# A long convolution in four FFT stages ahead of a wide MLP: an intermediate re-laid in blocks of four columns, the third stage one chunk later, deeper product buffers, one store for each tile of y

## The chip, the core and the metric

The kernel runs on one core of a Trainium2 chip. The metric is device microseconds of one execution; the median of three runs is compared. Engines: PE does matrix products (PEld is its weight load, which can run beside a product), DVE, ACT and POOL do elementwise work, SP issues all DMAs of this kernel in one queue. [...]

## The reference

```python
def _attn_ref(x, v, pos_emb, w1, w2):          # x, v: 4 x 12480 x 128
    h_mlp = np.maximum(pos_emb @ w1, 0.0) @ w2
    h_filt = h_mlp * np.exp(-0.01 * pos)[:, None]
    u = x * v
    Uf = np.fft.rfft(u, n=2 * S, axis=1)
    Hf = np.fft.rfft(h_filt, n=2 * S, axis=0)
    y = np.fft.irfft(Uf * Hf[None], n=2 * S, axis=1)[:, :S]
    return x * y

def _moe_ref(x, w_in, w_out):                  # w_in: 128 x 2048, w_out: 2048 x 128
    h = x @ w_in
    g = h * np.clip(h + 3.0, 0.0, 6.0) / 6.0
    return g @ w_out
```

The second function gets the output of the first. All of it is float32.

## The kernel before

The FFT of 12544 = 64 x 196 points is done as matrix products. The work falls into a filter part (the spectrum of h, kept in DRAM as `hd`), eight **periods** (one for each group g of 2 batches x 32 channels), a **last turn**, and the MLP ("MoE" in the code) over 98 tiles of 512 positions.

Each period works on a tensor `z` of 128 partitions x 99 frequencies (K2) x 128 columns; there are two, `z[0]` and `z[1]`, used by even and odd groups. The stages:

- **First stage** (L282, copied out by ACT at L294): 16 products for four columns, written to `z[:, :, col:col+4]`. A **visit** does four of these, 16 columns, for the group after the present one.
- **Second stage** (L301): 4 frequencies are one **chunk** (25 in a period, c = 0 to 24); the table `tab` is the stationary operand, `z[:, k, :]` the moving one.
- **Products**: ACT copies a swapped half (L499, L500), DVE multiplies by the filter spectrum `h` (L520 to L523) and POOL adds (L527) into the tile `pa`. POOL also multiplies x and v (L453).
- **Third stage** (L542, copied out by ACT at L550): the products of a chunk with the same `tab`, written back into `z[:, k, :]`. It follows the products by `LAG` chunks.
- **Back** (L557): four columns of `z` are transposed on PE; here `z[:, :, col]` is the stationary operand and the identity the moving one. ACT copies the result to `w` (L560). 32 backs of group g-1 lie in period g.
- **Fourth stage** (L574): for 16 columns, from `w`; ACT copies one half (L584), DVE makes `y` from both (L586), SP stores `y` to `yd` and two single rows to `ye` (L592, L595).

Every engine works in the order in which the program is written (`manual_schedule`). In a period, `chunk` issues products of c, third stage of c-LAG+1, the load of a later `tab` into the buffer that the third stage freed, and the second stage of c+1; then follow one or two backs, in most periods with steps of a decode of the MLP's weights on DVE (`weight`), and after each fourth back a fourth stage and a visit. The fourth stage pops the oldest entry of `pend`, so it is one group of 16 columns behind the backs; the one left over runs in chunk 0 of the next period. The tables have `NT` buffers, the spectra `h` four. `z` is copied out of the single PSUM bank `s3`; backs, first and fourth stages share four banks `ts`.

The MLP loads its tiles with two DMAs, `xt` and `yt` (L713, L728), multiplies them (L741), transposes on DVE, and runs six products for each of 16 blocks; L768 to L770 are the first layer, L803 to L807 the second.

Of the kernel before, what the change touches and what calls it, by code (L numbers as in the profile page):

```python
# [9 lines left out]
F32 = mybir.dt.float32  # L10
# [27 lines left out]
G = 32  # L38
# [22 lines left out]
LAG = 3  # L61
# [5 lines left out]
NT = 7  # L67
# [91 lines left out]
@with_exitstack  # L159
def hyena_moe(ctx, tc, x, v, xt, pos_emb, w1, w2, w_in, w_out, c_tab, d_tab, f_tab, g_tab, win_d, ident_d, out):  # L160
    nc = tc.nc
    P = 128

    dram = ctx.enter_context(tc.tile_pool(name="dram", bufs=1, space=DRAM))
    hd = [dram.tile([D // G // 2, P, K2, 2, G], F32, name=f"hd{h}") for h in range(2)]
    yd = [[dram.tile([NR, 4, 32, G // GH, N1, GH], F32, name=f"yd{b}_{k}") for k in range(2)] for b in range(B)]
    ye = dram.tile([len(REST), D // GH, N1, GH], F32, name="ye")
    wd = [dram.tile([2, P, DFF], F32, name=f"wd{i}") for i in range(2)]
    w_in = w_in.bitcast(I32).rearrange("p (q k c) -> q p k c", k=NW, c=2)
    w_out = w_out.bitcast(I32).rearrange("(q f p) (k c) -> q p f k c", f=NW // D, p=P, c=2)  # L170
    weights = [(w[q], wd[i][:, :, q * NW : (q + 1) * NW]) for i, w in enumerate((w_in, w_out)) for q in range(DFF // NW)]

    const = ctx.enter_context(tc.tile_pool(name="const", bufs=1))
    ident = const.tile([P, P], F32, name="ident")

    left, right = ExitStack(), ExitStack()
    with tc.manual_schedule():
        conv = Conv(tc, nc, left, right, x, v, c_tab, d_tab, g_tab, ident, hd, yd, ye, weights)
# [5 lines left out]
        moe = Moe(ctx, tc, nc, xt, wd, yd, ye, out)  # L184
        conv.last_turn(moe)
        right.close()
        moe.run()
# [64 lines left out]
class Conv:  # L252
    def __init__(self, tc, nc, left, right, x, v, c_tab, d_tab, g_tab, ident, hd, yd, ye, weights):
        self.tc, self.nc, self.left, self.right = tc, nc, left, right
        self.x, self.v, self.g_tab, self.ident, self.hd, self.yd = x, v, g_tab, ident, hd, yd
        self.c_tab, self.d_tab, self.weights, self.ye = c_tab, d_tab, weights, ye
# [4 lines left out]
        self.z = [self.keep.tile([128, K2, COLS], F32, name=f"z{i}") for i in range(2)]  # L261
# [12 lines left out]
    def first_stage(self, z, u, k, piece, j):  # L274
# [15 lines left out]
        dst, src = z[:, :K2, col : col + 4], tv[:, :, :K2].rearrange("p j k -> p k j")  # L290
# [5 lines left out]
    def second_stage(self, tab, z, c):  # L296
# [3 lines left out]
        for i in range(kw):  # L300
            self.nc.tensor.matmul(  # L301
                t[:, i * 128 : (i + 1) * 128], tab[:, i, :], z[:, c * CH + i, :], start=True, stop=True
            )
        return t, kw

    def filter(self, pos_emb, w1, w2, f_tab, win_d, ident_d):
        tc, nc = self.tc, self.nc
        z, ftab = self.z
# [15 lines left out]
        flat = z.rearrange("p k c -> p (k c)")  # L324
# [178 lines left out]
    def products(self, item):  # L503
# [5 lines left out]
        a = self.pr.tile([P, CH, 2 * GB, G], F32, tag="a", name="pa")  # L509
        a2 = self.pr.tile([P, CH, 2 * GB, G], F32, tag="a2", name="pa2", bufs=2)  # L510
        q = self.pr.tile([P, CH, GB, G], F32, tag="q", name="pq", bufs=2)
        q2 = self.pr.tile([P, CH, GB, G], F32, tag="q2", name="pq2", bufs=2)
# [23 lines left out]
    def third_stage(self, item):  # L536
# [13 lines left out]
        nc.scalar.copy(z[:, c * CH : c * CH + kw, :].rearrange("p k c -> p (k c)"), t[:, : kw * 128])  # L550

    def back(self, g, col):
# [11 lines left out]
    def fourth_stage(self):  # L564
# [24 lines left out]
        for h in range(2):  # L589
            e = ch // GH + h  # L590
            for i, p, q, r, n in PARTS:
                nc.sync.dma_start(self.yd[b][k][q, d // G, r : r + n, e], y[64 * h + p : 64 * h + p + n, i])  # L592
            for i, p, r in ((0, 49, 49), (1, 1, 97)):
                if r < R[k]:
                    nc.sync.dma_start(  # L595
                        self.ye[REST.index((b, k, r)), d // GH + e].unsqueeze(0), y[64 * h + p : 64 * h + p + 1, i]
                    )

    def period(self, g):
# [7 lines left out]
        for c in range(NCHUNK):  # L607
# [4 lines left out]
            while n < end:  # L612
# [4 lines left out]
                if n % VISIT == 0:  # L617
                    if n > VISIT:
                        self.fourth_stage()
                    if g + 1 < NG:  # L620
                        self.visit(g + 1, n // VISIT - 1)

    def chunk(self, g, c):
# [7 lines left out]
        if g > 1 and c == 0:  # L631
            self.fourth_stage()
# [39 lines left out]
class Moe:  # L672
# [7 lines left out]
    def __init__(self, ctx, tc, nc, x, wd, yd, ye, out):  # L680
        self.ctx, self.tc, self.nc = ctx, tc, nc
        self.x, self.yd, self.ye, self.out = x, yd, ye, out
# [26 lines left out]
    def load(self, t):  # L709
# [4 lines left out]
        if self.is_rest(t):  # L714
            i = self.tiles[t]
            s = REST.index(i[0])
            for j in range(4):
                for m in range(len(i)):
                    a = self.ye[s + m, 4 * j : 4 * j + 4].rearrange("e (h r) c -> r h e c", r=32)
# [5 lines left out]
        else:  # L725
            b, k, q, n = self.tiles[t]
            a = self.yd[b][k][q].rearrange("q r e n c -> (q r) e n c")[:, :, n : n + self.NB, :]
            nc.sync.dma_start(  # L728
                y.rearrange("p (e m) -> p e m", e=4), a.rearrange("p e n c -> p e (n c)")
            )  # L730
        self.loaded[t] = xt, y

# [142 lines left out]
```

## Time and profile before

| what | us |
|---|---|
| median of three runs (3252.92, 3256.47, 3272.07) | 3256.47 |
| the profiled execution | 3259.06 |
| its span | 3257.3 |
| PE busy in it | 3156.4 |
| DVE, ACT, POOL busy in it | 2315.7, 2356.5, 2079.7 |
| granted PE clock, mean | 0.992 |

The execution is the span and some 1.8 us around it. The filter part ends at 160.3 us, where the first period begins; the last turn ends at 1120.9, where the first product of the MLP starts. PE's share of 97% is a mean over these parts, which have different limits.

### The profile page before, as it was taken

To read this page: it belongs to the slowest core of one execution; us is meant where nothing else is said; L and a number is where in the kernel's file an instruction comes from. 1 tells how busy PE (TensorE), PEld (TensorE's weight loads), DVE (VectorE), ACT (ScalarE), POOL (GpSimd) and SP (SyncE) were. 2 spreads that over 40 slices of the span, in tenths; PEclk is the share of its full clock that TensorE was granted. 3 is DMA by queue.
4 is the path that set the end of the run, shared out by engine and by line. 5 is a ranking of instruction groups with operands and counts; after the bars stand their busy time and mean duration, and the time that the engine had idled before them with its cause. 6 is when DMAs were issued, how large, how long until landed. Compare 5 with 4: busy or idle time off the path is not lost.

```text
span 3257.3 us, 53858 instructions
## 1 busy us (share of the span) xinstructions
PE 3156.4 (97%) x20026; PEld 2667.5 (82%) x20026; DVE 2315.7 (71%) x2691; ACT 2356.5 (72%) x3039; POOL 2079.7 (64%) x1242
## 2 busy tenths in 40 slices
PE   9989899899899899999999999999999999999999
PEld 8988787787787588888888888888888888888887
DVE  4456676676656377777777777777777777777776
ACT  2356666666676577778877787778777877787777
POOL 1177767767767166666666666666666666666666
PEclk9999999999999999999999999999999999999999
DMA  6677777777765401011111111111111110111010
GB/s 232 198 202 193 206 194 196 206 200 193 203 173 168 141 30 39 30 36 39 39 39 34 36 39 39 33 36 40 39 30 39 39 39 30 39 39 39 30 39 23
DMA packets 236980, 296.70 MB, mean 91 GB/s; under 512 B 38727, under 2 KB 159854, under 8 KB 235694
## 3 DMA queue, kind: packets, MB, share of 16 engines
q1 hardware_dynamic: 236718, 293.26, 31.7%
q8 instruction: 158, 2.59, 0.3%
q14 instruction: 104, 0.85, 0.1%
HBM read 224.87 MB, written 68.29 MB: 90 GB/s over the span
## 4 chain that ended last, share of the span: by engine, by line
PE 66%; DMA 1%; SPq 0%; POOL 0%; ACT 0%; issue 0%; DVE 0%; DVEq 0%; ACTq 0%
PE acc L807 11%; PE acc L803 11%; PE acc L804 11%; PE ph L769 11%; PE ph L770 11%; PE ph L768 11%; DMA yd<-y 1%; PE ts L574 0%; PE ts L557 0%; SPq L592 0%; PE s L557 0%; DMA yt<-yd 0%; PE s L542 0%; PE s L301 0%; DMA ye<-y 0%; DMA tab<-in_g_tab 0%
## 5 line engine op out<-in xcount | busy, mean ns | idle before, releaser
L792 POOL TENSOR_TENSOR glo<-g,ghi 128x1024 fp32r<-128x1024 f32 x588 | 1404.3, 2396 | 775.4 <-ACT ghi L790 775.2
L780 DVE SCALAR_TENSOR_TENSOR g<-r,ph 128x1024 f32<-128x1024 f32 (+1 forms) x784 | 949.3, 1211 | 413.8 <-ACT r L778 413.6
L778 ACT ACTIVATE r<-ph,three 128x1024 f32<-128x1024 f32 (+1 forms) x784 | 871.4, 1112 | 277.6 <-PE ph L770 277.5
L790 ACT CAST ghi<-g 128x1024 fp32r<-128x1024 f32 (+1 forms) x784 | 811.1, 1035 | 5.4 <-DMA ye<-y 4.2
L768 PE MATMUL ph<-xhi,win_hi 128*128 128x512 f32 (+1 forms) x1568 | 609.1, 388 | 2.3 <-DVE y L586 2.3
L803 PE MATMUL acc<-ghi,wout_hi 128*128 128x512 f32 (+1 forms) x1568 | 608.6, 388 | 2.3 <-ACT ghi L790 2.3
L769 PE MATMUL ph<-xlo,win_hi 128*128 128x512 f32 (+1 forms) x1568 | 608.8, 388 | 0.0
L770 PE MATMUL ph<-xhi,win_lo 128*128 128x512 f32 (+1 forms) x1568 | 608.8, 388 | 0.0
L804 PE MATMUL acc<-ghi,wout_lo 128*128 128x512 f32 (+1 forms) x1568 | 608.6, 388 | 0.0
L807 PE MATMUL acc<-glo,wout_hi 128*128 128x512 f32 (+1 forms) x1568 | 481.8, 388 | 1.0 <-POOL glo L792 1.0
L527 POOL TENSOR_TENSOR pa<-pa,pq 128x256 f32<-128x256 f32 (+1 forms) x400 | 290.3, 732 | 247.4 <-DVE pa L521 220.8
L768 PEld LDWEIGHTS ph<-xhi,win_hi 128*128 128x128 f32 x1568 | 294.7, 188 | 64.2 <-issue 2.7
L803 PEld LDWEIGHTS acc<-ghi,wout_hi 128*128 128x128 f32 x1568 | 294.7, 188 | 63.4 <-ACT ghi L790 2.8
L807 PEld LDWEIGHTS acc<-glo,wout_hi 128*128 128x128 f32 x1568 | 294.0, 188 | 62.4 <-POOL glo L792 2.0
L770 PEld LDWEIGHTS ph<-xhi,win_lo 128*128 128x128 f32 x1568 | 294.6, 188 | 60.7
L804 PEld LDWEIGHTS acc<-ghi,wout_lo 128*128 128x128 f32 x1568 | 294.6, 188 | 60.6
L769 PEld LDWEIGHTS ph<-xlo,win_hi 128*128 128x128 f32 x1568 | 294.6, 188 | 60.5
L792 DVE TENSOR_TENSOR glo<-g,ghi 128x1024 fp32r<-128x1024 f32 x196 | 283.3, 1446 | 0.0
L520 DVE TENSOR_TENSOR pq<-s,h 128x256 f32<-128x256 f32 (+1 forms) x200 | 84.1, 420 | 280.0 <-POOL pa L527 124.3
L542 PE MATMUL s<-pa,tab 128*128 128x128 f32 x1694 | 242.3, 289 | 40.5 <-POOL pa L527 30.3
L542 PEld LDWEIGHTS s<-pa,tab 128*128 128x128 f32 x1694 | 212.4, 197 | 64.4 <-POOL pa L527 50.0
L741 DVE TENSOR_TENSOR xy<-xt,yt 128x512 f32<-128x512 f32 x96 | 260.3, 2711 | 0.0
(60 smaller groups left out, 3675.4 us busy)
## 6 DMA issues: line engine op xcount, KB each, us to landing
tab<-in_g_tab SPq DMA_DIRECT2D x192, 256.0 KB
h<-hd SPq DMA_DIRECT2D x384, 128.0 KB
xt<-in_xt SPq DMA_DIRECT2D x98, 256.0 KB
out<-o SPq DMA_DIRECT2D x97, 256.0 KB
xt<-in_x SPq DMA_DIRECT2D x64, 384.0 KB
vt<-in_v SPq DMA_DIRECT2D x64, 384.0 KB
yt<-yd SPq DMA_DIRECT2D x96, 256.0 KB
yd<-y SPq DMA_DIRECT2D x256, 64.0 KB
```

What stands on the lines that cost most here:

```text
L527: nc.gpsimd.tensor_tensor(out=x, in0=x, in1=y, op=add)
L542: nc.tensor.matmul(t[:, i * 128 : (i + 1) * 128], tab[:, i, :], a[:, i].rearrange("p s g -> p (s g)"), start=(n == 0), stop=(n == len(term ...
L768: nc.tensor.matmul(ph[:, i, :ne], self.win_hi[:, sl], hi[:, :ne], start=True, stop=False)
L769: nc.tensor.matmul(ph[:, i, :ne], self.win_hi[:, sl], lo[:, :ne], start=False, stop=False)
L770: nc.tensor.matmul(ph[:, i, :ne], self.win_lo[:, sl], hi[:, :ne], start=False, stop=True)
L778: nc.scalar.activation(r[:, :, :ne], ph[:, :, :ne], AF.Relu, bias=self.three)
L780: nc.vector.scalar_tensor_tensor(out=g[:, :, :ne], in0=r[:, :, :ne], scalar=6.0, in1=ph[:, :, :ne], op0=ALU.min, op1=ALU.mult)
L790: nc.scalar.copy(ghi[:, :, :ne], g[:, :, :ne])
L792: e.tensor_tensor(out=glo[:, :, :ne], in0=g[:, :, :ne], in1=ghi[:, :, :ne].bitcast(F32), op=ALU.subtract)
L803: nc.tensor.matmul(a, self.wout_hi[:, f, :], ghi[:, i, :ne], start=(f == 0), stop=False)
L804: nc.tensor.matmul(a, self.wout_lo[:, f, :], ghi[:, i, :ne], start=False, stop=False)
L807: nc.tensor.matmul(a, self.wout_hi[:, f, :], glo[:, i, :ne], start=False, stop=(f == NFC - 1))
```

## The change

- `z` has the shape 128 x 32 blocks x 99 frequencies x 4 columns. A column's 99 values, which the back loads as weights, lie 16 bytes apart and not 512; a frequency's 128 values, which the second stage reads and the third stage's copy writes, lie in 32 runs of four floats (16 for the copy of four frequencies) and not in one row. The first stage's copy writes one run of 396 floats.
- `LAG` is 4, not 3, and there are 8 tables, not 7. The product buffers `a2`, `q`, `q2` have three copies and not two, `a` four and not three; `w` has two and not three.
- The visit comes ahead of the fourth stage, the fourth stage runs from the first 16 columns on, and none is left for chunk 0 of the next period. In period 7, which has no visit, the fourth stage follows its last back directly.
- `y` is stored whole by one DMA, in the order in which it lies; `ye` is gone. The MLP gathers a tile of `yd` with four or eight DMAs of 32, 17 or 15 rows and not one of 128.

```diff
-LAG = 3
+LAG = 4
...
-NT = 7
+NT = 8
...
-    yd = [[dram.tile([NR, 4, 32, G // GH, N1, GH], F32, name=f"yd{b}_{k}") for k in range(2)] for b in range(B)]
-    ye = dram.tile([len(REST), D // GH, N1, GH], F32, name="ye")
+    yd = [[dram.tile([D // G, G // GY, 2 * 64, 2, N1, GH], F32, name=f"yd{b}_{k}") for k in range(2)] for b in range(B)]
...
-        self.z = [self.keep.tile([128, K2, COLS], F32, name=f"z{i}") for i in range(2)]
+        self.z = [self.keep.tile([128, COLS // 4, K2, 4], F32, name=f"z{i}") for i in range(2)]
...
-        dst, src = z[:, :K2, col : col + 4], tv[:, :, :K2].rearrange("p j k -> p k j")
+        dst, src = z[:, col // 4], tv[:, :, :K2].rearrange("p j k -> p k j")
...
-                t[:, i * 128 : (i + 1) * 128], tab[:, i, :], z[:, c * CH + i, :], start=True, stop=True
+                t[:, i * 128 : (i + 1) * 128], tab[:, i, :], z[:, :, c * CH + i, :], start=True, stop=True
...
-        a = self.pr.tile([P, CH, 2 * GB, G], F32, tag="a", name="pa")
-        a2 = self.pr.tile([P, CH, 2 * GB, G], F32, tag="a2", name="pa2", bufs=2)
-        q = self.pr.tile([P, CH, GB, G], F32, tag="q", name="pq", bufs=2)
-        q2 = self.pr.tile([P, CH, GB, G], F32, tag="q2", name="pq2", bufs=2)
+        a = self.pr.tile([P, CH, 2 * GB, G], F32, tag="a", name="pa", bufs=4)
+        a2 = self.pr.tile([P, CH, 2 * GB, G], F32, tag="a2", name="pa2")
+        q = self.pr.tile([P, CH, GB, G], F32, tag="q", name="pq")
+        q2 = self.pr.tile([P, CH, GB, G], F32, tag="q2", name="pq2")
...
-        nc.scalar.copy(z[:, c * CH : c * CH + kw, :].rearrange("p k c -> p (k c)"), t[:, : kw * 128])
+        nc.scalar.copy(z[:, :, c * CH : c * CH + kw, :], t[:, : kw * 128].rearrange("p (k q c) -> p q k c", k=kw, c=4))
...
-            nc.tensor.transpose(t[:K2, i * 128 : (i + 1) * 128], self.z[g % 2][:, :, col + i], self.ident)
+            nc.tensor.transpose(t[:K2, i * 128 : (i + 1) * 128], self.z[g % 2][:, col // 4, :, i], self.ident)
...
-            self.w = self.wp.tile([K2, GY, 128], F32, tag="w", name="w", bufs=3)
+            self.w = self.wp.tile([K2, GY, 128], F32, tag="w", name="w")
...
-        for h in range(2):
-            e = ch // GH + h
-            for i, p, q, r, n in PARTS:
-                nc.sync.dma_start(self.yd[b][k][q, d // G, r : r + n, e], y[64 * h + p : 64 * h + p + n, i])
-            for i, p, r in ((0, 49, 49), (1, 1, 97)):
...
+        nc.sync.dma_start(self.yd[b][k][d // G, ch // GY], y)
...
                 if n % VISIT == 0:
-                    if n > VISIT:
-                        self.fourth_stage()
                     if g + 1 < NG:
                         self.visit(g + 1, n // VISIT - 1)
+                    self.fourth_stage()
...
-        if g > 1 and c == 0:
-            self.fourth_stage()
...
             b, k, q, n = self.tiles[t]
-            a = self.yd[b][k][q].rearrange("q r e n c -> (q r) e n c")[:, :, n : n + self.NB, :]
-            nc.sync.dma_start(
-                y.rearrange("p (e m) -> p e m", e=4), a.rearrange("p e n c -> p e (n c)")
-            )
+            for i, p, block, r, m in PARTS:
+                for j in range(4 if block == q else 0):
+                    a = self.parts(b, k, j, i, p, p + m)[:, :, n : n + self.NB, :]
+                    nc.sync.dma_start(
+                        y[32 * j + r : 32 * j + r + m, :].rearrange("r (e m) -> r e m", e=4),
+                        a.rearrange("r e n c -> r e (n c)"),
+                    )
...
+    def parts(self, b, k, j, i, p0, p1):
+
+        return self.yd[b][k][j].rearrange("f (e p) i n c -> i p (f e) n c", p=64)[i, p0:p1]
```

Three places in the engines' order. First PE around one fourth stage in period 3: `s_...` is the result of a second or third stage, `pa` the products, `ts` the shared bank. Before:

```order
L557 MATMUL ts<-ident,z_79 99x128 x4
L574 MATMUL ts<-w,dtab 64x512 x4
L282 MATMUL ts<-ctab,u 64x99 x32
L557 MATMUL ts<-ident,z_79 99x128 x4
L542 MATMUL s_6905<-pa,tab 128x128 x4
```

After (the first stage is L281 there, the second L300):

```order
L557 MATMUL ts<-ident,z_78 99x128 x4
L281 MATMUL ts<-ctab,u 64x99 x32
L574 MATMUL ts<-w,dtab 64x512 x4
L542 MATMUL s_6538<-pa,tab 128x128 x4
L300 MATMUL s_6546<-z_79,tab 128x128 x4
```

The visit's products now stand between the last transposes and the fourth stage that takes their copy.

The second place is PE in period 7, the last one, around a fourth stage. Before:

```order
L301 MATMUL s_12705<-z_80,tab 128x128 x4
L557 MATMUL ts<-ident,z_79 99x128 x4
L574 MATMUL ts<-w,dtab 64x512 x4
L542 MATMUL s_12756<-pa,tab 128x128 x4
L301 MATMUL s_12764<-z_80,tab 128x128 x4
```

After:

```order
L300 MATMUL s_12230<-z_79,tab 128x128 x4
L557 MATMUL ts<-ident,z_78 99x128 x4
L574 MATMUL ts<-w,dtab 64x512 x4
L542 MATMUL s_12270<-pa,tab 128x128 x4
L300 MATMUL s_12278<-z_79,tab 128x128 x4
```

The rows look alike, but the `w` that L574 reads was filled 16 columns earlier before, and is filled by the copy of the transposes right ahead of it after; nothing else stands between.

The third place is SP around the stores of one fourth stage in a later period. Before:

```order
L471 DMA tab<-in_g_tab 128x512
L592 DMA yd_1_62<-y 32x512 x2
L592 DMA yd_1_62<-y 17x512
L592 DMA yd_1_62<-y 15x512
L595 DMA ye<-y 1x512
L592 DMA yd_1_62<-y 32x512 x2
L592 DMA yd_1_62<-y 17x512
L592 DMA yd_1_62<-y 15x512
L595 DMA ye<-y 1x512
L484 DMA h<-hd_57 64x2x256 x2
```

After:

```order
L484 DMA h<-hd_57 64x2x256 x2
L471 DMA tab<-in_g_tab 128x512
L589 DMA yd_1_62<-y 128x1024
L484 DMA h<-hd_57 64x2x256 x2
L471 DMA tab<-in_g_tab 128x512
```

Ten or twelve issues have become one.

## Rows read from the trace of the kernel before

**Rows 1.** Windows, stages: stretch, length, busy time by engine, clock, DMA share, GB/s

```profile
160.30:1120.90 960.60, 877.23 (x8398) 761.66 (x8398) 597.66 (x1106) 617.87 (x1160) 653.81 (x641) 0.98 0.71 191
1120.90:3257.30 2136.40, 2126.49 (x9409) 1760.61 (x9408) 1642.55 (x1371) 1687.37 (x1764) 1404.32 (x588) 1.00 0.12 37
```

**Rows 2.** Waits of PE from 160.3 to 1120.9: total us, times, longest

```profile
PE s L542 <- POOL pa L527: 30.3, 50, 1.8
PE s L301 <- DMA tab<-in_g_tab: 19.3, 12, 3.1
PE ts L557 <- DVE y L586: 16.0, 6, 3.5
PE s L542 <- ACT z L550: 7.6, 16, 1.5
PE s L301 <- DVE pa L521: 4.2, 2, 2.6
```

**Rows 3.** Windows: one whole period, and one stretch of lower clock

```profile
493.60:616.50 122.90, 110.79 (x1103) 97.04 (x1102) 83.53 (x149) 79.38 (x151) 86.89 (x83) 0.97 0.76 204
...
399.85:403.26 3.41, 3.37 (x16) 3.40 (x17) 3.34 (x7) 0.43 (x1) 2.80 (x3) 0.50 1.12 272
```

**Rows 4.** Timeline of PE around that stretch: start, length, idle before and its releaser

```profile
399.89 2.05 PE L301 MATMUL s<-z,tab 128*128 128x128 f32 x8 [3.10 <-DMA tab<-in_g_tab]
401.73 1.79 PE L557 MATMUL ts<-ident,z 128*99 128x128 f32 x8
...
404.25 1.06 PE L301 MATMUL s<-z,tab 128*128 128x128 f32 x8
405.14 0.84 PE L557 MATMUL ts<-ident,z 128*99 128x128 f32 x4
```

**Rows 5.** Lines by form, weight loads: busy us, mean ns, idle before

```profile
L557 PEld LDWEIGHTS ts<-ident,z 128*99 128x99 f32 x960 | 179.9, 262 | 20.7 <-DVE y L586 17.3 <-issue 1.6 <-ACT z L550 0.9
...
L357 PEld LDWEIGHTS h<-w2bd,ht 128*98 128x98 f32 x256 | 29.0, 165 | 0.4 <-issue 0.2
```

**Rows 6.** Timeline of PE in the last turn; the clock rises at 1079.1

```profile
1075.67 1.06 PE L557 MATMUL s<-ident,z 128*99 128x128 f32 x4
1076.52 1.06 PE L557 MATMUL ts<-ident,z 128*99 128x128 f32 x4
...
1081.61 0.84 PE L557 MATMUL s<-ident,z 128*99 128x128 f32 x4
1082.29 0.84 PE L557 MATMUL ts<-ident,z 128*99 128x128 f32 x4
```

**Rows 7.** Timeline of SP, stores of one fourth stage: first and last

```profile
429.05 1.58 SPq L592 DMA_DIRECT2D yd<-y  x4
...
433.66 0.51 SPq L595 DMA_DIRECT2D ye<-y  x2
```

**Rows 8.** Timeline near the end of period 3: a visit, then a wait

```profile
596.79 2.90 PE L282 MATMUL ts<-ctab,u 97*64 97x99 f32 x64
...
601.89 1.27 DVE L586 TENSOR_TENSOR y<-ts,o 128x512 f32<-128x512 f32 x2
...
603.22 0.95 PE L557 MATMUL ts<-ident,z 128*99 128x128 f32 x4 [3.53 <-DVE y L586]
```

**Rows 9.** Lines by form, copies by ACT: busy us, mean ns

```profile
L294 ACT COPY z<-ts 128x396 f32<-128x396 f32 x272 | 133.1, 489 | 96.3 <-PE ts L282 77.3 <-DMA xt<-in_x 14.9
...
L550 ACT COPY z<-s 128x512 f32<-128x512 f32 x192 | 111.9, 583 | 5.5 <-PE s L542 5.5
...
L378 ACT COPY st<-s 128x256 f32<-128x256 f32 x48 | 17.9, 372 | 41.4 <-PE s L301 30.8 <-DVE st L380 10.0 <-DMA tab<-in_g_tab 0.6
```

**Rows 10.** Timeline of PE where the MLP begins

```profile
1117.61 1.07 PE L574 MATMUL ts<-w,dtab 99*64 99x512 f32 x2 [1.82 <-ACT w L560]
...
1124.88 0.47 PE L768 MATMUL ph<-xhi,win_hi 128*128 128x512 f32 x1 [2.29 <-DVE y L586]
...
1133.00 0.50 PE L803 MATMUL acc<-ghi,wout_hi 128*128 128x512 f32 x1 [2.33 <-ACT ghi L790]
```

More of the change, by code (lines that the diff above doesn't have):

```diff
@@ L177, in hyena_moe @@
     with tc.manual_schedule():
-        conv = Conv(tc, nc, left, right, x, v, c_tab, d_tab, g_tab, ident, hd, yd, ye, weights)
+        conv = Conv(tc, nc, left, right, x, v, c_tab, d_tab, g_tab, ident, hd, yd, weights)
         conv.filter(pos_emb, w1, w2, f_tab, win_d, ident_d)
@@ L183, in hyena_moe @@
         left.close()
-        moe = Moe(ctx, tc, nc, xt, wd, yd, ye, out)
+        moe = Moe(ctx, tc, nc, xt, wd, yd, out)
         conv.last_turn(moe)
@@ L252, with __init__ @@
 class Conv:
-    def __init__(self, tc, nc, left, right, x, v, c_tab, d_tab, g_tab, ident, hd, yd, ye, weights):
+    def __init__(self, tc, nc, left, right, x, v, c_tab, d_tab, g_tab, ident, hd, yd, weights):
         self.tc, self.nc, self.left, self.right = tc, nc, left, right
         self.x, self.v, self.g_tab, self.ident, self.hd, self.yd = x, v, g_tab, ident, hd, yd
-        self.c_tab, self.d_tab, self.weights, self.ye = c_tab, d_tab, weights, ye
+        self.c_tab, self.d_tab, self.weights = c_tab, d_tab, weights
         self.loaded, self.gated, self.n_loaded = [], [], 0
@@ L307, in filter @@
         tc, nc = self.tc, self.nc
-        z, ftab = self.z
+        z = self.z[0]
+        ftab = self.z[1].rearrange("p q k c -> p (q k c)").rearrange("p (k c) -> p k c", k=K2)
         P = 128
@@ L322, in filter @@
         NB = 4
-        flat = z.rearrange("p k c -> p (k c)")
+        flat = z.rearrange("p q k c -> p (q k c)")
         pT = flat[:, : N1 * R[0]].rearrange("p (n r) -> p n r", r=R[0])
@@ L588, in fourth_stage @@
         k, b, d = self.place(g, piece)
-        for h in range(2):
-            e = ch // GH + h
-            for i, p, q, r, n in PARTS:
-                nc.sync.dma_start(self.yd[b][k][q, d // G, r : r + n, e], y[64 * h + p : 64 * h + p + n, i])
-            for i, p, r in ((0, 49, 49), (1, 1, 97)):
-                if r < R[k]:
-                    nc.sync.dma_start(
-                        self.ye[REST.index((b, k, r)), d // GH + e].unsqueeze(0), y[64 * h + p : 64 * h + p + 1, i]
-                    )
+        nc.sync.dma_start(self.yd[b][k][d // G, ch // GY], y)
     def period(self, g):
@@ L678, with __init__ @@
     NB = 16
-    def __init__(self, ctx, tc, nc, x, wd, yd, ye, out):
+    def __init__(self, ctx, tc, nc, x, wd, yd, out):
         self.ctx, self.tc, self.nc = ctx, tc, nc
-        self.x, self.yd, self.ye, self.out = x, yd, ye, out
+        self.x, self.yd, self.out = x, yd, out
         P = 128
@@ L714, in load @@
         if self.is_rest(t):
[L715 to L719, printed above, removed]
+            for m, (b, k, r) in enumerate(self.tiles[t]):
+                i, p = (0, r) if r < RH else (1, R[0] - r)
+                for j in range(4):
+                    a = self.parts(b, k, j, i, p, p + 1)[0].rearrange("e (h r) c -> r h e c", r=32)
                     for h in range(2):
@@ L726, in load @@
             b, k, q, n = self.tiles[t]
-            a = self.yd[b][k][q].rearrange("q r e n c -> (q r) e n c")[:, :, n : n + self.NB, :]
-            nc.sync.dma_start(
-                y.rearrange("p (e m) -> p e m", e=4), a.rearrange("p e n c -> p e (n c)")
-            )
+            for i, p, block, r, m in PARTS:
[5 more added lines that the diff above has]
+                    )
         self.loaded[t] = xt, y
+    def parts(self, b, k, j, i, p0, p1):
+        return self.yd[b][k][j].rearrange("f (e p) i n c -> i p (f e) n c", p=64)[i, p0:p1]
     def gate(self, t):
```

## The prediction, made before the changed kernel ran

> **What bounds the kernel now.** I read the windows by stage first. The MLP keeps PE busy 2126.5 of 2136.4 us, and none of its arithmetic is touched, so nearly all that can move lies in the 960.6 us of the periods and the last turn, where PE is busy 877.2 and idle 83.4 [rows 1]. Within a period of 122.9 us PE works 110.8, POOL 86.9, DVE 83.5, ACT 79.4, and the DMA engines are 0.76 busy, some 93 us [rows 3]. PE is the bound, with a second row of limits at 70 to 76% behind it. So a microsecond off PE's own work or off its waits shortens the run until the period comes near 93.
>
> The list of PE's waits then says what the 83.4 us are: 30.3 for the last POOL addition of a product, 19.3 for a table, 16.0 for DVE's y, 7.6 for the copy out of the single bank `s3`, 4.2 for a DVE product that still reads a second-stage bank [rows 2]. These five are 77.4 of the 83.4.
>
> The waits cost more than their length. After the 3.10 us wait for a table the granted clock is 0.50, the 1.2 GHz level, for 3.41 us [rows 3, 4]. Eight second-stage instructions take 1.84 us there (399.89 to 401.73) and 0.89 at the higher level (404.25 to 405.14) [rows 4]; four transposes take 0.85 and 0.68 [rows 6]. That stretch, eight of the one and eight of the other, cost 0.95 + 0.34 = 1.3 us. A period at a mean of 0.97 loses 3% of 122.9 us of full clock, so it has 7.4 us at the lower level, two such stretches [rows 3]. Six periods (1 to 6) read 0.97, so there are about twelve, some 16 us in all.
>
> **The third stage one chunk later, with the product buffers.** Products of c are issued ahead of third stage c-2 before, c-3 after, so POOL has one more chunk of PE time (period / 25, 4.9 us on average) to finish. The longest of its 50 waits is 1.8 us [rows 2], well under that. The added buffers are what lets DVE and POOL use the slack. I take 25 of 30.3 (15 to 30: POOL's work is not shortened, and where chunks carry no backs it can still be last). The 7.6 for `s3` stay, since that bank stays single; so do the 4.2.
>
> The moved third stage brings its copy with it. The third stage of a period's last chunk now runs in chunk 2 of the next, right ahead of the first back, which reads the copied column. Between them lies only a second stage of 0.89 us [rows 4] against a copy of up to 0.58 [rows 9] and its queue on ACT: +0.3 us in seven periods, +2 (0 to 5).
>
> **The visit ahead of the fourth stage, and no fourth stage in chunk 0.** The typical wait for y: the visit starts at 596.79 and is over at 599.7, DVE ends y at 603.16 and the next transposes, whose bank y still holds, start at 603.22 after 3.53 us idle [rows 8]. After the change the visit's 2.9 us lie ahead of the fourth stage, and two backs with a chunk behind it before such a bank comes round. DVE still has the same work there, so some of the wait can come back as one for its product: 13 of 16.0 saved (6 to 16).
>
> In periods 1 to 6 the visit covers the copy of `w` (0.59 us). In period 7 there is no visit, and eight fourth stages wait for the copy just issued. Here the last fourth stage of the last turn shows the price: 1.82 us, of which the copy is only a third, the rest ACT's queue [rows 10]. The floor is the copy, 0.6, and its signals. Queued behind the wait on PE are a third and a second stage, and POOL and DVE behind those. 1.25 us each, +10 (6 to 18).
>
> **Whole-tile stores.** The issues of one fourth stage hold SP from 429.05 to 434.17 [rows 7], and every load of `h` and `tab` behind them waits, eight times a period: 8 x 5.1 = 41 us of a period's 122.9. One issue there is 0.26 to 0.40 us (0.51 / 2, 1.58 / 4), so some 38 us of SP's time come free. The bytes stay the same, and the DMA engines at 0.76 are not relieved of them, so I take 11 of the 19.3 us for tables (4 to 19). The depth of prefetch does not change: one more table, held one chunk longer.
>
> At the MLP's start the second layer's first product waits 2.33 us for a copy by ACT [rows 10], which lies in memory that the last `y` gives up when its stores have landed, and these stores stand in SP's late queue. I take 3 us there (0 to 5); the wait of 2.29 for a PSUM bank stays. The MLP's gathers are three to seven issues more for each tile of 21.8 us (2136.4 / 98), with two tiles loaded ahead; PE's 99.5% leaves them no share: 0.
>
> **Fewer stretches at the lower clock.** With most of the waits of over 2 us gone, I take 9 of the 16 us (3 to 15).
>
> **z in blocks of four.** On the copies I put 0: 256, 396 and 512 elements take 0.372, 0.489 and 0.583 us, that is 0.82 ns for each added element [rows 9], though the middle one reads PSUM 512 bytes apart and writes in runs of four, and the other two do not. What the layout can change is the transposes. Their weight load is 99 columns that lie 512 bytes apart and takes 262 ns; 98 columns that lie in a row take 165 [rows 5]. And the transposes are held by that load: at the lower clock one takes 0.85/4 = 0.213 us, not far from a second-stage instruction (0.230), at the higher one 0.170 where that takes 0.111 [rows 4, 6]. An array at double clock would go twice as fast; something that does not follow the clock holds it at 0.170. If the load ran at the pace of one in a row, a transpose would take 0.111 and the 1024 of them would give 60 us.
>
> Does a step of 16 bytes read like one of 512, or like a row? No row shows it; both ends are 0 and 60 us. In both layouts no two of the wanted values are adjacent; adjacency is what the 165 ns load has and the 262 ns load lacks. I take the nearest row, the strided load: 0.
>
> [...]
>
> **The sum.** -25 + 2 - 13 + 10 - 11 - 3 - 9 + 0 = -49 us. The profiled execution is 3259.06, so it would be 3210; it lies 2.6 us over the median of three, so the median comes to 3256.5 - 49 = **3207 us** (-1.5%). With every term at its good end the sum is -85 + 6 = -79 (3177), at its bad end -28 + 23 = -5 (3251).
>
> **Rivals.** *The load at full pace.* The 16-byte step reads like a row. For it: it is the one thing that the new order of z changes for an operation held by its operand. Against it: above. Of the 60 us I count 50, since a period then comes to about 109 us with some 93 of DMA in it, which leaves less room for late tables: 3207 - 50 = 3157 (3147 to 3171). [...]
>
> *The waits only move.* DVE decodes weights in bursts, POOL and DMA stay as loaded as they are, and each wait that goes is replaced by the next in line. For it: five different releasers, and none of the engines does less. Against: none is over 76% in a period. Near the bad end of the sum: -5 to -25, 3240.
>
> *The second stage pays for the runs.* Its moving operand is now 32 runs of four values with jumps of 1584 bytes between them. If each run cost what a far step costs the weight load, (262 - 165) / 99 = 1 ns, an instruction would take 32 ns more; there are 1980 of them (198 in each of eight periods, 396 in the filter part), +63 us, and the time would be 3207 + 63 = 3270, slower than before. If every value paid, it would be four times that. It decides from 25 ns an instruction on (49 / 1980). Against it: nothing in the trace speaks for a price at the fourth value, and the copy by ACT in runs of four has none [rows 9].
>
> **How the numbers follow.** Chances: forecast 0.56, the load at full pace 0.29, waits only move 0.09, runs pay 0.06. A measurement of this kernel tells about 1% from no change, 33 us. Of the forecast about four fifths lie beyond that: faster 0.45 + 0.29 + 0.02 = 0.76; slower by over 1% 0.04, the dear half of the runs; within 1% 0.20. The range leaves out the lower edge of the second case and the upper tail of the others: 3147 to 3238. The forecast's own range is 3180 to 3235.
>
> **What would show it.** The weight load of L557 at 262 ns and four transposes in 0.68 us confirm the term of 0; 165 ns and 0.45 mean the first rival. The wait for POOL should be under 8 us, for y under 4, for tables under 13; new ones should stand in period 7 (L574 for ACT's copy, eight of 0.8 to 1.8 us). Period 3 should come to 115 to 117 us at a clock of 0.98 to 0.99, and the MLP begin near 1075. The second stage should keep 0.89 us for eight. The forecast is wrong if L557's load changes, if tables still wait after SP is free (then DMA bandwidth, not the queue, made them late), or if PE's wait for y comes back under DVE's products.

## The result, and the profile after

The changed kernel takes 3212.86 us (median of four runs, 3211.72 to 3214.58), the kernel before 3256.64 beside it (3252.92 to 3272.07): a ratio of **0.9857**, 95% interval [0.9825, 0.9889]. The profiled execution takes 3211.72 us, 47.3 less than the one before; the forecast of that step was 49.

The windows of the changed kernel by stage, then period 3 (columns as in [rows 1]):

```profile
159.17:1081.25 922.08, 872.49 (x8399) 754.79 (x8399) 592.69 (x1106) 610.40 (x1160) 652.96 (x641) 1.00 0.71 207
1081.25:3209.60 2128.35, 2123.59 (x9409) 1758.93 (x9408) 1640.62 (x1371) 1686.40 (x1764) 1404.15 (x588) 1.00 0.12 37
478.65:593.40 114.75, 108.81 (x1104) 95.13 (x1103) 82.13 (x150) 78.20 (x151) 86.93 (x84) 1.00 0.76 221
```

Against [rows 1] the periods and the last turn give 38.5 us and the MLP 8.1. PE's idle time there falls from 83.4 to 49.6 us (922.08 - 872.49). A period takes 114.75 for 122.9, and its clock reads 1.00 for 0.97 [rows 3]. This clock is the granted share: the traces of both kernels have two levels of it, 1.00 and 0.50. The stretches that the prediction and the expectations place at 1.2 GHz are those at 0.50; no trace shows a frequency. The DMA engines move more bytes in less time, 207 for 191 GB/s at the same share of 0.71: by the page the whole kernel moves 304.7 MB for 296.7, since a whole tile of `y` (512 KB) holds rows that the pieces left out (some 390 KB).

The waits of PE in that stretch (as in [rows 2]):

```profile
PE s L542 <- ACT z L550: 33.4, 50, 1.3
PE ts L557 <- ACT z L550: 9.0, 8, 1.3
PE s L300 <- DVE pa L521: 6.3, 7, 2.1
PE s L542 <- POOL pa L527: 0.8, 1, 0.8
```

The waits for POOL, for a table and for y are gone: 65.6 us of them but for 0.8, where the forecast had left 16.6. But the copy out of `s3`, 8.2 us before (7.6 in [rows 2] and 0.6 under L557), now holds PE for 42.4. The list of waits shows half of the waits replaced, not removed.

Where that wait sits is plain in the timeline of PE of the changed kernel, at the start of period 3:

```profile
481.00 1.06 PE L300 MATMUL s<-z,tab 128*128 128x128 f32 x8
483.11 1.13 PE L542 MATMUL s<-pa,tab 128*128 128x128 f32 x8 [1.05 <-ACT z L550]
...
486.42 0.91 PE L542 MATMUL s<-pa,tab 128*128 128x128 f32 x6 [1.28 <-ACT z L550]
...
489.53 0.99 PE L557 MATMUL ts<-ident,z 128*99 128x128 f32 x4 [1.31 <-ACT z L550]
```

ACT in the same stretch:

```profile
481.30 0.56 ACT L499 COPY sw<-s 64x512 f32<-64x512 f32 x1 [1.41 <-DVE pa L523]
481.89 0.57 ACT L500 ACTIVATE sw<-s 64x512 f32<-64x512 f32 x1
482.38 0.58 ACT L550 COPY z<-s 128x512 f32<-128x512 f32 x1
484.61 0.56 ACT L499 COPY sw<-s 64x512 f32<-64x512 f32 x1 [1.64 <-DVE pa L523]
...
487.92 0.56 ACT L499 COPY sw<-s 64x512 f32<-64x512 f32 x1 [1.64 <-DVE pa L523]
```

Read across the two. ACT's L499 starts every 3.31 us (481.30, 484.61, 487.92), each time after DVE's last product of the chunk before (L523, which reads the one `sw` bank that L499 overwrites). The copy L550 stands behind L499 and L500 in ACT's order. The next third stage needs the bank that L550 empties, so PE, which has some 2 us of work a chunk here (a third and a second stage), takes 3.3 us for it, too. These chunks have no backs or visits to fill the gap.

The new layout, lines by form (as in [rows 5, 9]):

```profile
L557 PEld LDWEIGHTS ts<-ident,z 128*99 128x99 f32 x960 | 188.9, 275 | 21.9 <-issue 11.4 <-ACT z L550 10.5
L293 ACT COPY z<-ts 128x396 f32<-128x396 f32 x272 | 132.3, 489 | 92.5 <-PE ts L281 77.2 <-DMA xt<-in_x 14.9
L550 ACT COPY z<-s 128x512 f32<-128x512 f32 x192 | 111.9, 583 | 3.9 <-PE s L542 3.9
```

PE in the last turn and at the MLP's start (as in [rows 6, 10]):

```profile
1073.57 0.89 PE L557 MATMUL ts<-ident,z 128*99 128x128 f32 x4
1074.30 0.89 PE L557 MATMUL s<-ident,z 128*99 128x128 f32 x4
...
1090.05 0.73 PE L802 MATMUL acc<-glo,wout_hi 128*128 128x512 f32 x2 [0.39 <-POOL glo L787]
```

The copies cost what they cost, to the nanosecond (489 and 583 ns in both kernels). The weight load became a little slower, 275 ns for 262, and four transposes take 0.73 us for 0.68. Where the MLP begins, the waits of 2.29 and 2.33 us [rows 10] are gone; in the kernel before, a stretch of 6.8 us at a granted clock of 0.50 (1133.7 to 1140.5) followed them, which is gone too.

Period 7, PE again, one of eight fourth stages:

```profile
965.16 2.93 PE L574 MATMUL ts<-w,dtab 99*64 99x512 f32 x8
```

SP, one store (as in [rows 7]):

```profile
365.99 0.38 SPq L589 DMA_DIRECT2D yd<-y  x1
```

The fourth stage there takes 2.93 us; with its visit ahead it takes 1.91. The one store holds SP for 0.38 us, where the twelve of [rows 7] held it for 5.1, the waits between them included.

### The profile page after: what moved, and what is told of

It reads as the page before. It is cut to its first block, busy times and chain, and to the rows that moved or that the text cites. A ratio compares the mean times of both kernels' runs of the same rounds, so it can differ in the third digit from the quotient of the medians.

```text
span 3209.6 us, 53638 instructions
## 1 busy us (share of the span) xinstructions
PE 3147.8 (98%) x20026; PEld 2658.5 (83%) x20026; DVE 2308.7 (72%) x2691; ACT 2348.0 (73%) x3039; POOL 2078.7 (65%) x1242
## 4 chain that ended last, share of the span: by engine, by line
PE 68%; ACT 0%; DVE 0%; POOL 0%; DMA 0%; issue 0%; ACTq 0%; DVEq 0%
PE acc L802 11%; PE acc L798 11%; PE acc L799 11%; PE ph L763 11%; PE ph L765 11%; PE ph L764 11%; PE ts L574 1%; PE ts L557 1%; PE s L557 0%; PE s L542 0%; PE s L300 0%; DMA yd<-y 0%; POOL glo L787 0%; ACT z L550 0%; DVE y L586 0%
## 5 line engine op out<-in xcount | busy, mean ns | idle before, releaser
L542 PEld LDWEIGHTS s<-pa,tab 128*128 128x128 f32 x1694 | 205.9, 192 | 80.7 <-POOL pa L527 42.4
L542 PE MATMUL s<-pa,tab 128*128 128x128 f32 x1694 | 233.9, 282 | 34.2 <-ACT z L550 33.4
L527 POOL TENSOR_TENSOR pa<-pa,pa 128x512 f32<-128x512 f32 (+1 forms) x186 | 236.7, 1273 | 14.6
```

Source lines behind the costliest of these rows:

```text
L527: nc.gpsimd.tensor_tensor(out=x, in0=x, in1=y, op=add)
L542: nc.tensor.matmul(t[:, i * 128 : (i + 1) * 128], tab[:, i, :], a[:, i].rearrange("p s g -> p (s g)"), start=(n == 0), stop=(n == len(term ...
```

## The experiments

Four parts were changed: layout, third stage (with buffers), order, stores. The first question is which of them carries the 47 us. Times are medians, each with its ratio to the kernel before on the same chip. The diffs are cut to the lines that name the edit; the lines that follow from it are left out.

**One part alone, on the kernel before.** The layout:

```diff
-        self.z = [self.keep.tile([128, K2, COLS], F32, name=f"z{i}") for i in range(2)]
+        self.z = [self.keep.tile([128, COLS // 4, K2, 4], F32, name=f"z{i}") for i in range(2)]
```

> The kernel before with the new layout of z alone. Theory (the near step costs 12 ns a transpose): 3257 + 12 = 3269 us (3262 to 3274), load of L557 275 ns. Rival (the step is not the cause): 3257 (3253 to 3261), load 262. Whichever holds, the 33 us and more that the change gave don't come from the layout: if they did, this run would be at 3215.

3261.46 us, 1.0002 [0.9992, 1.0011]. The load is 275 ns here too, and the transposes work some 10 us longer, but PE idles 4.5 us less; the time does not move. So the load is the theory's and the time, within its interval, the rival's.

The stores:

```diff
-                nc.sync.dma_start(self.yd[b][k][q, d // G, r : r + n, e], y[64 * h + p : 64 * h + p + n, i])
...
+        nc.sync.dma_start(self.yd[b][k][d // G, ch // GY], y)
```

> The kernel before with nothing but the whole-tile stores of y, without the tensor of single rows, and the MLP gathers that go with them. The changed kernel with the old stores stood at 1.0006, so the other three parts together gave nothing there. Theory: these parts shift the bound to the tables, which come late only under the old stores, so the stores alone remove what is late for that reason and leave the waits of the rest: table waits 19.3 to under 3 us, ghi at the MLP's start 2.3 to about 1, POOL's 30 and y's 16 stay, about half of the 48 us at 1.2 GHz goes: ratio 0.989 to 0.993. Rival: the stores are the whole change, and worth the same 48 us here: ratio 0.984 to 0.987.

3214.72 us, **0.9857** [0.9842, 0.9872]: the number of the rival, and the whole gain of the change. Windows by stage:

```profile
160.36:1084.78 924.42, 869.80 (x8399) 753.58 (x8399) 599.02 (x1106) 615.34 (x1160) 654.62 (x641) 0.99 0.72 207
1084.78:3213.13 2128.35, 2123.37 (x9409) 1759.26 (x9408) 1640.79 (x1371) 1687.36 (x1764) 1405.05 (x588) 1.00 0.12 37
```

PE's waits in the first of them (lines are one lower here):

```profile
PE s L541 <- POOL pa L526: 26.4, 46, 1.8
PE s L541 <- ACT sw L498: 13.8, 6, 2.3
...
PE ts L556 <- DVE y L585: 4.5, 10, 0.9
```

The table waits are gone (19.3 before), POOL's stay as the theory had it, and the MLP part is as short as in the changed kernel. What the theory had wrong is y: 16.0 fell to 4.5 with PE's order untouched. In the kernel before, DVE's own waits in these parts show y held back 19.8 us in five places by earlier stores that still held its tile; here it has none:

```profile
DVE y L586 <- DMA yd<-y: 16.3, 4, 6.7
DVE y L586 <- DMA ye<-y: 3.5, 1, 3.5
```

The third stage:

```diff
-LAG = 3
+LAG = 4
...
-NT = 7
+NT = 8
```

> The kernel before with nothing but the third stage three chunks behind the products, eight tables, and the new numbers of product buffers and of w. Taking this part out of the changed kernel cost 0.9939 against 0.9857, 27 us. Theory: under the old stores PE that no longer waits for POOL runs into late tables: POOL's waits fall from 30 to under 4 us, those for a table rise from 19 to over 28, ratio 0.997 to 1.003. Rival: the part is worth its 27 us by itself: ratio 0.990 to 0.993, waits for a table at 19 or less.

3254.65 us, 0.9985 [0.9974, 0.9996], as the theory said. The three main waits of PE:

```profile
PE s L301 <- DMA tab<-in_g_tab: 30.8, 19, 3.1
PE s L542 <- ACT z L550: 16.4, 35, 1.3
PE ts L557 <- DVE y L586: 12.3, 6, 3.2
```

POOL's 30.3 us are down to 0.8, and 11.5 of them came back as later tables, 15.3 as waits for the s3 copy (23.5 with the 7.1 that stand under L557, for 8.2).

**One part taken out of the changed kernel.** The stores:

```diff
-        nc.sync.dma_start(self.yd[b][k][d // G, ch // GY], y)
+                nc.sync.dma_start(self.yd[b][k][q, d // G, r : r + n, e], y[64 * h + p : 64 * h + p + n, i])
```

> The changed kernel with the old stores of y in pieces, the single rows in a tensor of their own, and the old gathers of the MLP; everything else stays changed. Theory: the ten issues of each fourth stage made the tables late, and the long waits for tables are what lowered the granted clock. Then waits for a table come back to 12 to 25 us, several stretches at 1.2 GHz with them (20 us or more in all), and the MLP's start gets its 2 us wait for ghi back: ratio 0.991 to 0.997 (changed kernel 0.9857). Rival: DMA bandwidth and the depth of prefetch made them late, so that the eighth table is what removed the waits: ratio 0.985 to 0.988, waits for tables under 5 us.

3263.58 us, **1.0006** [0.9996, 1.0016], beyond what the theory allowed: without the stores the other three parts together give nothing. No wait for y is left here, under the old stores. The longest row of PE's waits (lines are one higher here):

```profile
PE s L301 <- DMA tab<-in_g_tab: 34.8, 19, 3.7
```

SP ahead of two late tables:

```profile
366.69 1.47 SPq L593 DMA_DIRECT2D yd<-y  x4
...
369.88 0.54 SPq L472 DMA_DIRECT2D tab<-in_g_tab  x1
...
375.60 0.34 SPq L472 DMA_DIRECT2D tab<-in_g_tab  x1
```

PE where it uses them:

```profile
372.97 1.13 PE L301 MATMUL s<-z,tab 128*128 128x128 f32 x8 [0.91 <-DMA tab<-in_g_tab]
...
378.77 2.05 PE L301 MATMUL s<-z,tab 128*128 128x128 f32 x8 [3.60 <-DMA tab<-in_g_tab]
```

There are 200 issues of a table and 200 second stages, in the same order. By that count the table used at 378.77 was issued at 375.60, and the one at 372.97 at 369.88: PE takes a table as soon as it lands, about 3 us after its issue. From the end of the issue to the use it is never under 6.6 us in the changed kernel and as short as 2.5 here (periods 1 to 7), though there are eight tables in both; with the stores alone, and seven tables, it is never under 6.4. So the late tables come from the place in SP's queue, not from the depth of prefetch or from bandwidth.

The queue lost more than the time of the issues. From the first period to the MLP the stores of `y` hold SP for 223 us in the kernel before and for 23 in the changed one. Besides, the list of SP's waits before has 132 us (194 waits) in which SP stands until an earlier transfer has landed, often one that the store behind it does not need; with the changed kernel it is 20 us (31 waits), with the stores alone 25. In the run here one of 1.4 us, for an `xt`, stands right ahead of the issue at 375.60. The longest row of the kernel before:

```profile
SPq L592 <- DMA vt<-in_v: 24.5, 25, 1.8
```

Why a store waits for the landing of `vt` is not shown. Nor does a run keep the many issues but store the tile in its new place, so that the number of issues and the new form of the stores are not told apart.

The third stage:

```diff
-LAG = 4
+LAG = 3
...
-NT = 8
+NT = 7
```

> The changed kernel with the third stage two chunks behind the products again, seven tables and the old numbers of product buffers; layout, order of visit and fourth stage, and stores stay changed. Theory: the later third stage only exchanged one wait for another (POOL 30.3 to 0.8 us, copy out of s3 8.2 to 42.4), because ACT's copies of the swapped half and DVE's products form a loop of 3.3 us a chunk that bounds PE there whatever stands behind. Then POOL's waits come back to 20 to 30 us, the waits for the s3 copy fall under 15, and the time stays within 0.3% of the changed kernel: ratio to before 0.983 to 0.989 (changed kernel 0.9857). Rival, the prediction's own term: it is worth 23 us, ratio 0.992 to 0.994, with the waits for the s3 copy still near 40.

3240.02 us, 0.9939 [0.9924, 0.9954]. The time is the rival's, the prediction's own term; the waits for POOL and for the s3 copy are much as the theory had them, not near 40 for the copy as the rival had. PE's waits:

```profile
PE s L542 <- POOL pa L527: 32.6, 37, 1.8
PE s L542 <- ACT z L550: 15.0, 27, 1.2
PE s L542 <- ACT sw L499: 13.5, 6, 2.3
```

The theory fails as a mere exchange because a wait for `sw` stands here too: the later third stage takes away 45.3 us of waits (POOL 31.8, `sw` 13.5) and gives back 26.8 for the s3 copy and 4.4 for a DVE product. Idle time differs by 16.2 us (65.8 for 49.6). Clock makes up most of the rest: 27.3 us at a granted clock of 0.50, where the changed kernel has 3.4. In period 3, for instance, PE waits 2.25 us for `sw` up to 505.34, and from 506.0 to 509.4 the granted clock is 0.51.

The order:

```diff
+                    if n > VISIT:
+                        self.fourth_stage()
                     if g + 1 < NG:
                         self.visit(g + 1, n // VISIT - 1)
-                    self.fourth_stage()
...
+        if g > 1 and c == 0:
+            self.fourth_stage()
```

> The changed kernel with the fourth stage ahead of the visit and one group of 16 columns behind again, the left-over one in chunk 0 of the next period; layout, third stage, buffers and stores stay changed. Theory: the order removed the waits for y. Then the waits of L557 for DVE's y come back to 10 to 16 us in six places, with some stretch of the lower clock, and period 7 gives back its 6 to 8 us of waits for the copy of w: ratio 0.986 to 0.990 (changed kernel 0.9857). Rival: the chunks of slack in the later third stage and the freed SP already let DVE be early with y, so the order only costs period 7: ratio 0.982 to 0.984, waits for y under 4 us.

3199.16 us, 0.9812 [0.9793, 0.9831]: some 14 us **faster** than with the new order, on the rival's side and a little past it. The intervals of the two ratios overlap by 0.0006, so the two profiles have to carry the reading. PE at the start of period 3, to be held against that of the changed kernel:

```profile
478.84 1.13 PE L542 MATMUL s<-pa,tab 128*128 128x128 f32 x8 [0.17 <-ACT z L550]
479.90 1.94 PE L574 MATMUL ts<-w,dtab 99*64 99x512 f32 x8
481.77 1.16 PE L300 MATMUL s<-z,tab 128*128 128x128 f32 x8
```

The left-over fourth stage, 1.94 us of work, stands just where PE otherwise waits for the loop of ACT and DVE. Waits for the s3 copy are 24.3 us for 42.4, those for y 6.9 for 0. Period 7 takes 84.9 us for 92.6; the last turn takes 57.3 for 52.4, at a clock of 0.88.

The layout:

```diff
-        self.z = [self.keep.tile([128, COLS // 4, K2, 4], F32, name=f"z{i}") for i in range(2)]
+        self.z = [self.keep.tile([128, K2, COLS], F32, name=f"z{i}") for i in range(2)]
```

> The changed kernel with z laid out as before (one row of 128 columns for each frequency), all else as changed. Theory: in the changed kernel the 16-byte step reads slower than the 512-byte step (weight load of the transposes 275 ns against 262, a transpose every 182 ns against 170), so the new layout costs 1024 x 12 ns = 12 us. Then this run takes about 3201 us (3198 to 3206), its load is 262 ns and four transposes take 0.68 us again. Rival: the longer load comes from the denser DMA traffic or the like and not from the step, or the layout gives as much elsewhere; then this run is at 3213 (3209 to 3217) and its load stays near 275.

3209.05 us, 0.9841 [0.9825, 0.9857]: the load is the theory's, back at 261 ns, and the time the lower edge of the rival's, not told apart from the changed kernel. The transposes take 9 us less from start to start, but PE idles 3 us more, and 10.2 us of the last turn are at a granted clock of 0.50.

**The step of the weight load by itself.** Blocks of two columns, then of one (a column in a row, the second stage's values 396 bytes apart), all else as changed:

```diff
-        self.z = [self.keep.tile([128, COLS // 4, K2, 4], F32, name=f"z{i}") for i in range(2)]
+        self.z = [self.keep.tile([128, COLS // 2, K2, 2], F32, name=f"z{i}") for i in range(2)]
```

> The changed kernel with blocks of two columns: a column's values 8 bytes apart, the second stage's moving operand in 64 runs of two. Theory (what counts is two wanted values in each stretch of 16 bytes): the load falls to about 165 ns, four transposes to 0.45 us, 1024 x 71 ns = 73 us less PE work, of which some is lost to other limits: 3213 - 50 to 73 = 3140 to 3163 us. Rival (any step over one value is slow): load 262 to 290 ns, 3205 to 3225 us. If the second stage's eight instructions take over 0.89 us, the runs of two cost the moving operand something.

> The changed kernel with one column to a block: a column's 99 values in a row, the second stage's moving operand 396 bytes apart at each value. The load should be 165 ns and four transposes 0.45 us, -73 us. Theory A (the moving operand pays for a far step as the load does, 0.111 to 0.213 us an instruction): 1980 x 0.10 = +202 us, 3213 - 73 + 202 = 3342 us. Theory B (the moving operand is not held by the step): 3213 - 50 to 73 = 3140 to 3163 us.

Blocks of two: 3186.35 us, 0.9775 [0.9761, 0.979]. Blocks of one: 3328.64, 1.0208 [1.0193, 1.0223]. Lines by form in blocks of two:

```profile
L557 PEld LDWEIGHTS ts<-ident,z 128*99 128x99 f32 x960 | 116.4, 169 | 21.8 <-issue 11.4 <-ACT z L550 10.4
L300 PE MATMUL s<-z,tab 128*128 128x128 f32 x1584 | 216.4, 278 | 11.8 <-DVE pa L521 11.1 <-issue 0.7
```

The same in blocks of one:

```profile
L557 PEld LDWEIGHTS ts<-ident,z 128*99 128x99 f32 x960 | 130.0, 173 | 28.3 <-issue 11.4 <-ACT z L550 5.5
L300 PE MATMUL s<-z,tab 128*128 128x128 f32 x1584 | 406.6, 414 | 2.5 <-DVE pa L521 1.8 <-issue 0.7
```

At a step of 8 bytes the load takes 169 ns, near the 165 of 98 columns in a row [rows 5], and a transpose starts every 0.109 us, not 0.182. The transposes then work 68 us less, but PE idles 29 us more (78.4), most of it for the s3 copy: 60.7 us for 42.4. So the time lies between the two expectations. Where the second stage itself steps 396 bytes it is busy nearly twice as long (406.6 us, 211.5 in runs of four), and pays far more than the transposes save, nearly as theory A had it.

**The loop of ACT and DVE.** A second bank for `sw`, taken from the shared four:

```diff
-    BANKS = {"s2": 2, "sw": 1, "s3": 1, "ts": 4}
+    BANKS = {"s2": 2, "sw": 2, "s3": 1, "ts": 3}
```

> The changed kernel with two PSUM banks for the swapped half of the second stage (sw) and three, not four, shared by backs, first and fourth stages (ts). Theory: at the start of a period the single sw bank ties ACT's copies of chunk c to DVE's products of chunk c-1, 3.3 us a chunk, and the copy out of s3 stands behind them in ACT's queue. With a second bank the waits of L542 and L557 for that copy fall from 42 us to under 15, the waits for ts do not grow by more than 5: ratio 0.977 to 0.981 (changed kernel 0.9857). Rival: DVE's four products (2.2 us a chunk) and POOL bound these chunks anyway, or three ts banks make backs and visits wait: ratio 0.985 or more, with the idle time moved to DVE pa, POOL or ts.

3179.51 us, **0.9754** [0.9739, 0.9768], the theory's side and a little past it. The same start of period 3, PE:

```profile
472.85 1.13 PE L542 MATMUL s<-pa,tab 128*128 128x128 f32 x8
473.81 1.06 PE L300 MATMUL s<-z,tab 128*128 128x128 f32 x8
474.82 0.91 PE L542 MATMUL s<-pa,tab 128*128 128x128 f32 x6
```

ACT there:

```profile
473.01 0.56 ACT L499 COPY sw<-s 64x512 f32<-64x512 f32 x1 [0.31 <-PE s L300]
...
474.90 0.56 ACT L499 COPY sw<-s 64x512 f32<-64x512 f32 x1 [0.23 <-PE s L300]
```

L499 comes every 1.89 us here (474.90 - 473.01), and what it waits for is PE, not DVE. Waits for the s3 copy are 6.7 us for 42.4.

**Towards a better kernel.** Two columns, the second `sw` bank and the old order together:

```diff
+        self.z = [self.keep.tile([128, COLS // 2, K2, 2], F32, name=f"z{i}") for i in range(2)]
...
+    BANKS = {"s2": 2, "sw": 2, "s3": 1, "ts": 3}
...
+                    if n > VISIT:
+                        self.fourth_stage()
```

> The changed kernel with three edits that the runs so far speak for: z in blocks of two columns, two banks for sw and three for ts, and the fourth stage ahead of the visit and one group behind as it was. Theory: two columns take 68 us of PE's transposes away, the second sw bank lifts the loop between ACT and DVE that used up 29 of them in runs of two, the order gives another 10: the period comes to about 101 us, ratio 0.953 to 0.963. Rival: with POOL at 86 us a period and the DMA engines near 91, the next limit (tables, POOL or y) takes half of it: ratio 0.964 to 0.972, idle PE time over 50 us.

3200.65 us, 0.9814 [0.9795, 0.9833]: slower than two columns or the second bank alone, a plain miss. PE's two longest waits tell why:

```profile
PE ts L281 <- DVE y L586: 23.2, 6, 5.1
PE ts L557 <- DVE y L586: 15.1, 5, 3.0
```

In the old order y holds one of now three shared banks when the visit or the next back wants it, and the periods have 72 us at a granted clock of 0.50. So the new order was tried with the other two:

```diff
+        self.z = [self.keep.tile([128, COLS // 2, K2, 2], F32, name=f"z{i}") for i in range(2)]
...
+    BANKS = {"s2": 2, "sw": 2, "s3": 1, "ts": 3}
```

> The changed kernel with z in blocks of two columns and with two banks for sw and three for ts; the order of visit and fourth stage stays the changed one. The same two edits with the old order stood at 0.9814 with 38 us of waits for y and 72 us at 1.2 GHz; each edit by itself at 0.9775 and 0.9754. Theory: the waits for y there came from the old order alone, in which y holds one of only three shared banks when the next transposes or the visit want it. Then waits for y are under 4 us here, waits for the s3 copy under 25 (60.7 in runs of two), 1.2 GHz under 10 us: ratio 0.957 to 0.967, at most what the two give added (27 + 34 us, 0.967). Rival: three banks are too few once the transposes run in 0.109 us, whatever the order: waits for ts over 20 us, ratio 0.970 to 0.980.

3140.13 us (3139.28 to 3142.57), **0.9645** [0.9629, 0.9661], the fastest of all, and as the theory had it. Windows of the periods with the last turn, and of period 3:

```profile
160.90:1008.60 847.70, 807.18 (x8398) 684.77 (x8398) 598.62 (x1106) 619.53 (x1160) 649.21 (x641) 1.00 0.80 225
459.90:566.80 106.90, 100.84 (x1103) 86.35 (x1103) 83.29 (x150) 79.72 (x151) 86.45 (x84) 1.00 0.84 238
```

No wait for y, and 40.5 us idle in all: 17.0 for a DVE product, 12.8 for the s3 copy, 7.0 for tables. The new order, a loss in the changed kernel, is a gain here: these two kernels differ in it alone.

## Why the prediction came out as it did

The time was right, 3213 for 3207, and the sign. The working behind it was right only in part: the term of the stores was three times too small, the order cost time where it was to save some, and the two errors made up for each other. That the sum came within 6 us is in good part luck. By its own signs the forecast held for tables and y, but the load of L557 did change (275 ns), which it had named as a sign of being wrong; period 3 took 114.75 us at a clock of 1.00, not 115 to 117 at 0.98 to 0.99, and the MLP began at 1081, not near 1075.

**The stores** were put at -14 us (-11 for tables, -3 at the MLP). Alone they give 44 us in the trace: 36.2 in the periods (960.6 to 924.42) and 8.1 in the MLP. I had counted SP's time rightly (38 us a period; by SP's rows 200 us of issues and 112 of waits for landings came free in the eight) and then left 8.3 of the 19.3 us of table waits standing, on the ground that the bytes stay the same and the DMA engines at 0.76 get no relief. That step failed: the table waits are gone at the same share of DMA time, and with 8 MB more to move, since each table is issued sooner. What hung on the same queue and was booked elsewhere is y: 11.5 of its 16 us go with the stores. At the MLP's start the wait of 2.29 us, which was to stay, went too.

The **clock** term (-9) was too small as well. 47.8 us of the periods and the last turn were at a granted clock of 0.50, 27.3 with the new stores, 3.4 with everything. Of the thirteen such stretches before, eleven begin within 2 us of the end of a PE wait of 2.2 to 3.5 us and two of one of 1.7 or 1.8; one table wait of 2.6 us (up to 523.8) has no such stretch. Second and third stages, whose instructions are unchanged, are busy 17 us less in the changed kernel (220.3 + 242.3 to 211.5 + 233.9).

**The later third stage** was put at -25, with +2 for the copy it takes along. POOL's wait went as said (30.3 to 0.8). Beside the other changed parts it is worth 27 us; on the kernel before, 4 (3258.81 - 3254.65). The step that failed is the copy: its waits of 7.6 were to stay and +2 to come, and they rose by 34. I looked for them only at the first back, and had not followed ACT's own wait for DVE, which holds the copy once the POOL wait is out of the way. The second bank for `sw` showed that this is the cause.

**The order** was put at -13 and +10 for period 7, together -3. Taken out of the changed kernel, it gives a kernel that is some 14 us faster (0.9812 for 0.9857). The cause given for the y wait [rows 8], the place of the visit, was not the only one: the new stores alone leave 4.5 us of 16.0, and under the old stores it is 12.3 with the old order (the third stage alone) and none with the new. Beside the new stores the order has only 6.9 us left to save. And a fourth stage that had covered PE's idle time in chunk 0 lost its place there, a cover that I did not look for. **Period 7**: against the stores alone (85.9 and 52.08 us) period 7 and the last turn take 92.6 and 52.35, so +7 for +10.

**The layout** was put at 0, with the load at 262 ns. The load took 275, and the time does not show it (1.0002 alone). The rival of a load at full pace is refuted for a step of 16 bytes: 275 ns. It is true of one of 8 bytes: 169. The four steps that were run, 4, 8, 16 and 512 bytes, gave 173, 169, 275 and 261 to 262 ns. The theory of the blocks of two had its load, 169 ns for 165; its stretch of 16 bytes is an assumption that is not shown beyond these four steps. Why 16 bytes is 13 ns slower than 512 is not shown either.

**The rival of the runs** is refuted as well: the second stage keeps its pace in runs of four (an instruction every 0.111 to 0.112 us in both kernels). **The rival of waits that only move** named the right danger and the wrong size: 34 of the 65.6 us moved to ACT's copy. How third stage, order and layout come to nothing together over the stores alone, when taken out one by one they read -27, +14 and +5, stays open by some 8 us, which these intervals, 5 to 10 us either way, do not settle.

## What to carry to other kernels

When several loads share one queue with small stores, cost the stores by what stands behind them: here one store for ten or twelve gave 44 us, more than any other single edit. Look at what the issuing engine itself waits for, too. Before a wait is removed, follow the next engine's own wait one step further, here from PE to ACT's copy to DVE's product, and look at what fills PE's time in the chunks that have little work. Parts that lift limits in series have no value of their own: undo each in the changed kernel and do each alone, since the two gave 27 and 4 us for the same edit.

## What the runs showed that was not expected

A weight load of 99 columns takes 262 ns at a step of 512 bytes, 275 at 16, 169 at 8 and 173 in a row: here the near step of 16 bytes is worse than the far one. The moving operand is indifferent to runs of four and nearly so to runs of two (busy 210.8 us in rows, 211.5 and 216.4 in these runs, for the 1584 second-stage instructions of the periods), and its time nearly doubles at 396 bytes a value (406.6). ACT's copy writes runs of four as fast as a row (583 ns), runs of two in 601, single values in 653. The many waits for the s3 copy of 1.3 us at most left the granted clock of the changed kernel's periods at 1.00 (3.4 us at 0.50 in all); the shorter list of waits for tables, of up to 3.1, came with stretches at 0.50. SP, the issuing engine, stood 132 us for landings before and 20 after, so the price of a small store was more than its issue here.
